# Pooled attention and a maxout network: when the third and fourth batches' queries are turned by DMA, and when the fourth k is folded

## The chip, the cores and the metric

The kernel runs on one core of one Trainium2 chip. The metric is the device time of one execution in microseconds, as a median of several runs. The profile is of one execution; its span is a little shorter than the device time.

A core has TensorE (PE, matrix products, with PEld for its weight loads), VectorE (DVE), ScalarE (ACT), GpSimd (POOL) and SyncE (SP). Each takes its instructions in the order of the program and waits for semaphores of others. DMA transfers are issued here by GpSimd (all loads but the first k), by SP (stores, and transposes during a DMA) and in one place by ScalarE.

## The reference

There are 8 batches of 8 heads, 576 positions and 64 dimensions. Keys and values are averaged over groups of 8 positions, so each head has 72 keys. Attention with these is followed by a network whose hidden layer is the largest of three products.

```python
k_p = k.reshape(B, H, Sp, pool, D).mean(axis=3)      # Sp = 72, pool = 8
v_p = v.reshape(B, H, Sp, pool, D).mean(axis=3)
scores = scale * np.matmul(q, k_p.transpose(0, 1, 3, 2))
attn = softmax(scores)                               # written out in the reference
attn_out = np.matmul(attn, v_p)

x = attn_out.transpose(0, 2, 1, 3).reshape(B * S, H * D)      # 4608 x 512
h = np.maximum(np.maximum(x @ w1, x @ w2), x @ w3)            # 4608 x 768
return h @ w_out                                              # 4608 x 512
```

## The kernel before

The network works on blocks of 512 rows (`block(n, ...)`, n from 0), while the attention of a later batch is woven in between its products. A block is a row of slots: each slot is one product of the network, and a plan says which attention steps follow it. In the steps, b is the batch (0 is the first): `q0` to `q3` turn a quarter or so of the queries on TensorE, `T` turns all of a batch's queries in one DMA transpose, `k` turns the folded keys, `s0` to `s7` are the scores of a head, `v` the products with the values, `x` turns their result.

```python
def load_q(b):
    qbs[b] = ld.tile([128, 4, NG, D], BF16, name="qb", tag="qb")     # two buffers
    src = ...
    n = 2 if b == 0 else 4
    for i in range(0, 4, n):
        nc.gpsimd.dma_start(out=qbs[b][:, i:i + n], in_=src[:, i:i + n])

def fold(e, t, out, dtype=F32):          # sums of 8, in three steps
    ...
    e.tensor_tensor(out=f, in0=t[:, :, 0:4, :], in1=t[:, :, 4:8, :], op=ALU.add)
    e.tensor_tensor(out=f[:, :, 0:2, :], in0=f[:, :, 0:2, :], in1=f[:, :, 2:4, :], op=ALU.add)
    e.tensor_tensor(out=out, in0=f[:, :, 0, :], in1=f[:, :, 1, :], op=ALU.add)

def turn_q(b, n0, n1, evac, tag):
    ...
    for n in range(n0, n1):
        nc.tensor.transpose(pqt[:, n - n0, :], qf[:, 128 * n:128 * n + 128], ident)   # line 182
    evac(out=qTs[b][:, n0:n1, :], in_=pqt)                                            # line 184

def turn_k(b):
    pkt = keys(b, ...)                   # three transposes, line 189
    for par, evac in enumerate((nc.vector.tensor_copy, nc.scalar.copy)):
        for odd in range(2):
            (evac if b > 2 else nc.vector.tensor_copy)(      # line 198; up to b = 2 all four on VectorE
                out=kz_all[b % 2][par][64 * par:64 * par + 64, :, 0:Sp]...[:, :, :, :, odd],
                in_=pkt[64 * odd:64 * odd + 64]...)

def score(b, h, out, tp, i0, i1):
    f = NG * (h // 2) + tp
    n = f // 2
    nc.tensor.matmul(out, kz_all[b % 2][f % 2][:, h, :],                              # line 207
                     qTs[b][:, n + i0:n + i1, 64 * (h % 2):64 * (h % 2) + 64], ...)

def scores(b, h):                        # two products, of kz of even and of odd parity
    psc = psum([128, 1024], F32, name="psc", tag="att", bufs=2)
    score(b, h, psc[:, 192:512], 0, 0, 5)
    score(b, h, psc[:, 512:768], 1, 0, 4)
    exp(ets[b][:, h, :], psc[0:Sp, 192:768])

# in do(b, steps):
    elif name[0] == "T":
        qTs[b] = sb2.tile([128, 2 * NG, 128], BF16, name="qT", tag="qT")
        nc.sync.dma_start_transpose(                                                  # line 289
            out=qTs[b], in_=qbs[b].rearrange("p hp t d -> p (hp t d)"))

def hidden_part(n, jc, c0, c1, hT):
    for wi in range(1, 3):
        pw = psum([128, c1 - c0], F32, name=f"pw{wi}", tag="pw", bufs=3)
        for kc in range(KCH):
            mm = nc.tensor.matmul(pw, w_sb[wi][...], xT[:, kc, col], ...)             # line 346
        if wi == 1:
            nc.scalar.activation(out=t, in_=pw, func=FT.Relu)
        else:
            nc.vector.tensor_tensor(out=hT[:, jc, c0:c1], in0=t, in1=pw, op=ALU.max)  # line 354
        yield                            # end of a slot
```

In block 1 the slots 0 to 11 are products of 256 columns, 12 to 17 of 512; then come eight slots of the output (lines 391 and 395). The even ones of the hidden slots are emptied by ScalarE, the odd ones by VectorE.

Of the kernel before, what the change touches and what calls it, by code (L numbers as in the profile page):

```python
# [14 lines left out]
def kernel(  # L15
# [11 lines left out]
    nc = tc.nc  # L27
# [37 lines left out]
    kts, vts, qbs, kps, qTs, ets = {}, {}, {}, {}, {}, {}  # L65

    def after(loads, first):
        for x in loads:
            tc.add_manual_dep(x.ins, first.ins.name, mybir.DependencyInfo(
                mybir.DependencyClass.Sync, mybir.DependencyReason.DATA),  # L70
                reason="weights first")
# [10 lines left out]
    def load_v(b, eng, dtype=F16, cuts=(0, H)):  # L82
        if b == 0:
            vts[0] = ld.tile([96, 4096], dtype, name="vt0", tag="vt")[:, 0:3072].rearrange(
                "p (h i d) -> p h i d", h=H, i=6)
            src = v[0].rearrange("h (p i) d -> p h i d", i=6)
            return [eng.dma_start(out=vts[0][:, h:g], in_=src[:, h:g])
                    for h, g in zip(cuts, cuts[1:])][-1]
        vts[b] = ld.tile([Sp, H, POOL, D], dtype, name="vt", tag="vt")
        src = v[b].rearrange("h (sp j) d -> sp h j d", j=POOL)  # L90
        return [eng.dma_start(out=vts[b][:, h:g], in_=src[:, h:g])
                for h, g in zip(cuts, cuts[1:])][-1]

    def load_q(b):
        qbs[b] = ld.tile([128, 4, NG, D], BF16, name="qb", tag="qb")
        src = q[b].rearrange("h s d -> (h s d)").rearrange(
            "(hp p t d) -> p hp t d", hp=4, p=128, t=NG)
        n = 2 if b == 0 else 4
        for i in range(0, 4, n):
            nc.gpsimd.dma_start(out=qbs[b][:, i:i + n], in_=src[:, i:i + n])  # L100

    w_sb = [const.tile([128, KCH, DFF], F16, name=f"mw{wi}", tag=f"mw{wi}")
            for wi in range(3)]
# [19 lines left out]
    for sign in (1, -1):  # L123
        nc.gpsimd.affine_select(
            out=pick, in_=pick, compare_op=ALU.is_ge, fill=0.0, base=7 * (sign < 0),
            pattern=[[sign, 6], [-8 * sign, 128]], channel_multiplier=6 * sign)
    for i in range(3):
        load_w(slice(256 * i, 256 * i + 256))
    nc.gpsimd.dma_start(
        out=wo_sb, in_=moe_w_out.rearrange("(jc p) c -> p jc c", p=128))  # L130
# [16 lines left out]
    def fold(e, t, out, dtype=F32):  # L147
        part, n = t.shape[:2]
        f = const.tile([part, n, 4, D], dtype, name="half" if dtype == F32 else "halfh",
                       tag="half" if dtype == F32 else "k16")  # L150
        e.tensor_tensor(out=f, in0=t[:, :, 0:4, :], in1=t[:, :, 4:8, :], op=ALU.add)  # L151
        e.tensor_tensor(out=f[:, :, 0:2, :], in0=f[:, :, 0:2, :], in1=f[:, :, 2:4, :],  # L152
                        op=ALU.add)
        e.tensor_tensor(out=out, in0=f[:, :, 0, :], in1=f[:, :, 1, :], op=ALU.add)

    def new_kp(b):
        kps[b] = sb2.tile([96, 6, D], BF16, name="kp", tag="kp")

    def fold_k(b, e, i0=0, i1=6):
        if b not in kps:  # L160
            new_kp(b)
        fold(e, kts[b][:, i0:i1], kps[b][:, i0:i1], F16 if e is nc.vector else F32)

    def fold_v(b):
        fold(nc.gpsimd, vts[b], vp_all[:, b, :, 0:D])
# [9 lines left out]
    def turn_q(b, n0, n1, evac, tag):  # L175
        if b not in qTs:
            qTs[b] = sb2.tile([128, 2 * NG, 128], BF16, name="qT", tag="qT")
        pqt = psum([128, n1 - n0, 128], BF16, name="pqt", tag=tag[0],
                       bufs=tag[1])
        qf = qbs[b].rearrange("p hp t d -> p (hp t d)")  # L180
        for n in range(n0, n1):
            nc.tensor.transpose(pqt[:, n - n0, :], qf[:, 128 * n:128 * n + 128],  # L182
                                ident)
        evac(out=qTs[b][:, n0:n1, :], in_=pqt)  # L184
# [9 lines left out]
    def turn_k(b):  # L194
        pkt = keys(b, ATT if len(pools) < 3 else SC)
        for par, evac in enumerate((nc.vector.tensor_copy, nc.scalar.copy)):
            for odd in range(2):
                (evac if b > 2 else nc.vector.tensor_copy)(  # L198
                    out=kz_all[b % 2][par][64 * par:64 * par + 64, :, 0:Sp].rearrange(
                         "p h (r i t) -> p h r i t", i=3, t=2)[:, :, :, :, odd],  # L200
                     in_=pkt[64 * odd:64 * odd + 64].rearrange("p i (h r) -> p h r i", r=12))
# [12 lines left out]
    def new_et(b):  # L214
        ets[b] = sb2.tile([Sp, H, S], F16, name="et", tag="et")
# [57 lines left out]
    PW = ("pw", 3)  # L273

    QS = ((0, 5), (5, 10), (10, 14), (14, 18))
    xns, mms = {}, []

    def do(b, steps):

        for name in steps.split():
            i = int(name[1:] or 0)
            if name[0] in "qQ":
                turn_q(b, *QS[i], nc.vector.tensor_copy if name[0] == "Q"
                       else nc.scalar.copy, TR)
            elif name[0] == "T":
                qTs[b] = sb2.tile([128, 2 * NG, 128], BF16, name="qT", tag="qT")
                nc.sync.dma_start_transpose(
                    out=qTs[b], in_=qbs[b].rearrange("p hp t d -> p (hp t d)"))  # L290
            elif name[0] == "k":
                turn_k(b)
            elif name[0] == "K":
                fold_k(b, nc.vector)
            elif name[0] == "s":
                if i == 0:
                    new_et(b)
                (scores if len(pools) < 3 else scores_flat)(b, i)
            elif name[0] == "d":
                sub_w(i)  # L300
            elif name[0] == "z":
                for par in range(2):
                    nc.vector.memset(kz_all[1][par], 0.0)
            elif name[0] == "w":
                turn_w(i, nc.scalar.copy if i % 2 else nc.vector.tensor_copy)
            elif name[0] == "v":
                xns[b, i] = values(b, CHUNKS[i][0])
            else:
                turn_x(b, *CHUNKS[i], xns[b, i], TR if b == 1 else ATT,
                       nc.vector.tensor_copy if name[0] == "X" else nc.scalar.copy)  # L310
# [4 lines left out]
    def sub_w(i, j0=0, j1=2, wi=(1, 2)):  # L315

        part = slice(256 * i + 128 * j0, 256 * i + 128 * j1)
        for t in [w_sb[w] for w in wi]:
            nc.vector.tensor_tensor(out=t[:, :, part], in0=t[:, :, part],  # L319
                                    in1=w_sb[0][:, :, part], op=ALU.subtract)  # L320
# [177 lines left out]
    def block(n, plan, parts, folds=()):  # L498

        for slot, _ in enumerate(part for stage in parts for part in stage(n)):  # L500
            if slot == 0 and n > 0:
                pool_work(n, mms[-1])
            for b, steps in plan.get(slot, ()):
                if b < B:
                    do(b, steps)
            if folds and slot in FOLDS:
                next(folds.pop(0))
# [3 lines left out]
              17: [(1, "K")], 24: [(1, "q0 k")], 25: [(1, "q1")],  # L511
              26: [(1, "s0 q2")], 27: [(1, "s1 s2")], 28: [(1, "s3 Q3")],
              29: [(1, "s4 s5")], 30: [(1, "s6 s7")], 31: [(1, "v0")],
              32: [(1, "v1 x0")], 33: [(1, "X1 v2 v3")]}, (hidden, project))
    load_k(3, nc.gpsimd)
    load_v(3, nc.gpsimd)
    load_q(3)
    fold_k(2, nc.gpsimd)
    fold_v(2)


    def plan1():
        return {1: [(1, "x2")], 2: [(1, "v4")], 3: [(1, "x3")],
                5: [(1, "x4")],
                6: [(2, "k")], 7: [(2, "q0")], 9: [(2, "q1")], 11: [(2, "q2 s0")],
                12: [(2, "s1 q3")], 13: [(2, "s2")], 14: [(2, "s3")], 15: [(2, "s4"), (3, "T")],
                16: [(2, "s5")], 18: [(2, "s7")],
                19: [(2, "v0")],
                20: [(2, "v1 x0")], 21: [(2, "v2 x1")], 22: [(2, "v3 x2")],
                23: [(2, "v4 x3")], 24: [(2, "x4"), (4, "T")], 17: [(2, "s6")]}  # L530
# [6 lines left out]
        got[14 if n == 2 else 13].append((b + 2, "T"))  # L537
        return got

    FOLDS_OF = {1: "k3 v3", 2: "k4 v4 k5", 3: "v5 k6 v6", 4: "k7 v7"}  # L540

    def pool_work(n, mm):

        if n + 3 < B:
            if n == 1:
                load_q(4)
            after([load_k(n + 3, nc.gpsimd)], mm)
            load_v(n + 3, nc.gpsimd)
            if n > 1:
                load_q(n + 3)  # L550
        for name in FOLDS_OF.get(n, "").split():
            if name[0] == "k":
                fold_k(int(name[1]), nc.gpsimd)
            else:
                fold_v(int(name[1]))
# [231 lines left out]

    folds = [f for wi in range(1, 3) for f in [fold_w(wi)] * 4]
    block(1, plan1(), (hidden, project))
    for n in range(2, 5):  # L790
        block(n, with_keys(n) if n == 5 - 1 else plan(n),
              (hidden, project))
# [50 lines left out]
```

The softmax here doesn't subtract the row's maximum and nothing guards it: scores larger than these inputs give would overflow.

## Time and profile before

| | before |
|---|---|
| device time, median of 3 | 230.81 us (230.67 to 230.87) |
| span of the profile | 229.0 us |
| TensorE busy | 219.8 us, 96% |
| VectorE busy | 130.5 us, 57% |
| ScalarE busy | 122.6 us, 54% |
| GpSimd busy | 140.0 us, 61% |
| moved by DMA | 33.52 MB |

The page gives for each engine its busy time and its share of the span. A second part follows the chain of work that ended last from the last instruction back to the first; the share of an engine in it tells more than its busy time. The timeline prints, in order of time, the start and the length of merged instructions, the engine, the line of the kernel, what is written and what is read, and in brackets how long the engine stood idle before and what ended that. A name such as `DMA_TRANSPOSE` on SPq is the time of issue on the queue; the time to landing is given apart.

### The profile page before, as it was taken

What the parts mean: (1) busy time and instruction counts of PE and PEld (TensorE: products, weight loads), DVE (VectorE), ACT (ScalarE), POOL (GpSimd) and SP (SyncE); (2) the same over time, 40 slices, a digit from 0 to 9 for tenths busy, and PEclk for the clock granted to TensorE, in tenths of its full rate; (3) what the DMA queues carried; (4) which work ended last, traced back from release to release, by engine and by line L of the source; (5) the groups of instructions that cost most, each with busy time, mean ns of one, the idle gap of its engine ahead of it and who ended that gap; (6) DMA issues with size and microseconds to landing.
All of it is one profiled execution on the core that took longest, in us unless ns stands there. A gap on an engine that the chain in (4) does not pass through costs nothing.

```text
span 229.0 us, 4411 instructions
## 1 busy us (share of the span) xinstructions
PE 219.8 (96%) x1686; PEld 134.9 (59%) x1687; DVE 130.5 (57%) x246; ACT 122.6 (54%) x221; POOL 140.0 (61%) x115
## 2 busy tenths in 40 slices
PE   7888999999999999999999999999999999999992
PEld 2477645568655545544554455455677667786682
DVE  3668876048426423632363236368578887897830
ACT  2277425756864586238623852683776435465330
POOL 7975201999959999999999759900343443920020
PEclk9999999999999999999999999999999999999999
DMA  6999999999569999986998799941421534301326
GB/s 172 208 197 197 211 202 208 194 177 225 106 110 216 221 161 212 159 194 119 223 153 199 127 218 189 190 110 24 92 53 40 121 71 87 84 11 46 76 68 183
DMA packets 47157, 33.52 MB, mean 146 GB/s; under 512 B 27104, under 2 KB 41888, under 8 KB 47136
## 3 DMA queue, kind: packets, MB, share of 16 engines
q0 software_dynamic: 16944, 16.98, 46.0%
q1 hardware_dynamic: 30032, 16.13, 32.2%
q8 instruction: 13, 0.21, 0.4%
q10 hardware_dynamic: 160, 0.13, 0.2%
q14 instruction: 8, 0.07, 0.1%
HBM read 34.60 MB, written 9.44 MB: 192 GB/s over the span
## 4 chain that ended last, share of the span: by engine, by line
PE 88%; DVE 6%; ACT 3%; issue 2%; DVEq 0%; ACTq 0%
PE pw L346 23%; PE po L395 18%; PE po L391 11%; PE pA L733 7%; PE psc L207 6%; PE pav L255 4%; PE pC L733 3%; PE wm L413 3%; PE pm L333 2%; PE oA L670 2%; PE pB L733 2%; DVE kz L198 2%; PE pqt L182 2%; DVE xn L263 2%; ACT kz L198 2%
## 5 line engine op out<-in xcount | busy, mean ns | idle before, releaser
L346 PE MATMUL pw<-xT,mw 128*128 128x512 f16 (+1 forms) x336 | 73.1, 349 | 0.4 <-ACT xT L249 0.2
L395 PE MATMUL po<-mwo,hT 128*128 128x512 f16 (+1 forms) x198 | 46.8, 373 | 0.0
L354 DVE TENSOR_TENSOR hT<-t,pw 128x512 f16<-128x512 f16 (+1 forms) x42 | 25.5, 610 | 36.7 <-ACT et L212 22.3
L346 PEld LDWEIGHTS <-mw 128*128 128x128 f16 x336 | 31.6, 98 | 21.5 <-DVE mw L319 0.6
L400 ACT COPY osb<-po 128x512 f32<-128x512 f32 (+1 forms) x32 | 18.5, 579 | 41.2 <-PE po L395 41.1
L212 ACT ACTIVATE et<-psc 72x576 f16<-72x576 f32 (+2 forms) x54 | 35.2, 660 | 7.1 <-PE psc L207 6.9
L151 POOL TENSOR_TENSOR half<-vt 72x2048 f32<-72x2048 f16 x7 | 28.4, 4060 | 14.1 <-DMA vt<-in_v_dram 13.7
L391 PE MATMUL po<-wm,xT 128*128 128x512 f16 (+1 forms) x132 | 33.0, 372 | 0.3 <-ACT osb L400 0.3
L352 ACT ACTIVATE t<-pw 128x512 f16<-128x512 f32 (+1 forms) x42 | 22.5, 537 | 13.4 <-PE pw L346 11.6
L263 DVE TENSOR_TENSOR xn<-pav,rcp 128x512 f16<-128x512 f32 x40 | 27.7, 691 | 1.6 <-DVE rcp L261 0.2
L395 PEld LDWEIGHTS <-hT 128*128 128x128 f16 x198 | 18.5, 98 | 16.3
L152 POOL TENSOR_TENSOR half<-half 72x1024 f32<-72x1024 f32 (+1 forms) x13 | 27.3, 2097 | 1.0
L207 PE MATMUL psc<-qT,kz 128*128 128x320 bf16 (+2 forms) x120 | 22.9, 278 | 1.8 <-DVE qT L184 0.9
L207 PEld LDWEIGHTS <-kz 128*128 128x128 bf16 x143 | 13.1, 98 | 14.7 <-ACT kz L198 2.0
L151 POOL TENSOR_TENSOR half<-ktFalse 96x1536 f32<-96x1536 f16 x6 | 18.6, 3099 | 4.3 <-DMA ktFalse<-in_k_dram 4.1
L255 PEld LDWEIGHTS <-et 72*128 72x128 f16 x320 | 15.4, 98 | 7.6 <-issue 0.3
L739 ACT CAST pad<-pA 128x512 f16<-128x512 f32 x27 | 15.3, 587 | 8.4 <-PE pA L733 6.0
L261 DVE RECIPROCAL rcp<-pav 128x8 f32<-128x8 f32 x40 | 8.2, 206 | 18.1 <-PE pav L255 17.9
L391 PEld LDWEIGHTS <-xT 128*128 128x128 f16 x132 | 12.1, 98 | 9.4 <-issue 0.4
L255 PE MATMUL pav<-vp,et 72*128 72x65 f16 x320 | 17.0, 194 | 0.1
L714 DVE SCALAR_TENSOR_TENSOR hT<-pad 128x512 f16<-128x512 f16 x18 | 14.4, 810 | 1.8 <-ACT pad L743 1.4
L733 PEld LDWEIGHTS <-sw 128*128 128x128 f16 x144 | 13.7, 98 | 2.7
(106 smaller groups left out, 279.2 us busy)
## 6 DMA issues: line engine op xcount, KB each, us to landing
out_dram<-osb SPq DMA_DIRECT2D x62, 128.0 KB, 3.2
ktFalse<-in_k_dram POOLq DMA_DIRECT2D x7, 576.0 KB, 6.6
qb<-in_q_dram POOLq DMA_DIRECT2D x7, 576.0 KB, 13.2
vt<-in_v_dram POOLq DMA_DIRECT2D x7, 576.0 KB, 10.9
mw<-in_moe_w_dram POOLq DMA_DIRECT2D x9, 256.0 KB, 9.2
ktTrue<-in_k_dram SPq DMA_DIRECT2D x3, 384.0 KB, 5.0
mwo<-in_moe_w_out_dram POOLq DMA_DIRECT2D x1, 768.0 KB, 13.2
qb<-in_q_dram POOLq DMA_DIRECT2D x2, 288.0 KB, 7.8
```

What stands on the lines that cost most here:

```text
L151: e.tensor_tensor(out=f, in0=t[:, :, 0:4, :], in1=t[:, :, 4:8, :], op=ALU.add)
L152: e.tensor_tensor(out=f[:, :, 0:2, :], in0=f[:, :, 0:2, :], in1=f[:, :, 2:4, :], op=ALU.add)
L207: nc.tensor.matmul(out, kz_all[b % 2][f % 2][:, h, :], qTs[b][:, n + i0:n + i1, 64 * (h % 2):64 * (h % 2) + 64], start=True, stop=True)
L212: nc.scalar.activation(out=out, in_=in_, func=FT.Exp, scale=1.0 / 64.0)
L255: nc.tensor.matmul(pav[:, h // 4, 65 * (h % 4):65 * (h % 4) + 65], ets[b][:, h, c0:c0 + 128], vp_all[:, b, h, :], start=True, stop=True)
L263: nc.vector.tensor_tensor(out=xn, in0=pv[:, :, :, 0:D], in1=rcp.to_broadcast([128, 2, 4, D]), op=ALU.mult)
L346: mm = nc.tensor.matmul(pw, w_sb[wi][:, kc, bass.ts(jc, 128)], xT[:, kc, col], start=(kc == 0), stop=(kc == KCH - 1))
L352: nc.scalar.activation(out=t, in_=pw, func=FT.Relu)
L354: nc.vector.tensor_tensor(out=hT[:, jc, c0:c1], in0=t, in1=pw, op=ALU.max)
L391: nc.tensor.matmul(po, xT[:, kc, bass.ts(m, 128)], wm_sb[:, kc, c], start=(kc == 0), stop=False)
L395: nc.tensor.matmul(po, hT[:, jc, bass.ts(mm, 128)], wo_sb[:, jc, c], start=False, stop=(jc == JCH - 1))
L733: mm = nc.tensor.matmul(p[:, w], a[:, kc, bass.ts(g, 128)], b[:, kc, :], start=(i in FIRST and w + kc == 0), stop=(w + kc == 2), skip_grou ...
```

## The change

The queries of the third batch (b = 2), which TensorE turned in four groups in block 1, are turned by one DMA transpose, issued by SP in block 0. The loads of the fourth batch are put behind it: the query load waits until that transpose has landed, and the k and v loads follow on the same queue. The fold of the third k comes ahead of these loads. The DMA transpose of the fourth batch (b = 3) waits until the v load has landed, and the query load of the fifth waits for that transpose. So both transposes run at times when no load is under way. To make room for these waits, GpSimd's work of block 1 is written down at slot 16 rather than at slot 0, and the fold of the fourth k is taken out of it and put ahead of the loads of the fifth batch. The key turn of the third batch moves from slot 6 to slot 7.

```diff
--- before.py
+++ after.py
@@ -96,8 +96,8 @@
         src = q[b].rearrange("h s d -> (h s d)").rearrange(
             "(hp p t d) -> p hp t d", hp=4, p=128, t=NG)
         n = 2 if b == 0 else 4
-        for i in range(0, 4, n):
-            nc.gpsimd.dma_start(out=qbs[b][:, i:i + n], in_=src[:, i:i + n])
+        return [nc.gpsimd.dma_start(out=qbs[b][:, i:i + n], in_=src[:, i:i + n])
+                for i in range(0, 4, n)][-1]
 
     w_sb = [const.tile([128, KCH, DFF], F16, name=f"mw{wi}", tag=f"mw{wi}")
             for wi in range(3)]
@@ -273,7 +273,7 @@
     PW = ("pw", 3)
 
     QS = ((0, 5), (5, 10), (10, 14), (14, 18))
-    xns, mms = {}, []
+    xns, mms, turned = {}, [], {}
 
     def do(b, steps):
 
@@ -286,8 +286,10 @@
                        else nc.scalar.copy, TR)
             elif name[0] == "T":
                 qTs[b] = sb2.tile([128, 2 * NG, 128], BF16, name="qT", tag="qT")
-                nc.sync.dma_start_transpose(
+                turned[b] = nc.sync.dma_start_transpose(
                     out=qTs[b], in_=qbs[b].rearrange("p hp t d -> p (hp t d)"))
+                if b == 3:
+                    after([turned[b]], last_v)
             elif name[0] == "k":
                 turn_k(b)
             elif name[0] == "K":
@@ -498,7 +500,7 @@
     def block(n, plan, parts, folds=()):
 
         for slot, _ in enumerate(part for stage in parts for part in stage(n)):
-            if slot == 0 and n > 0:
+            if slot == (16 if n == 1 else 0) and n > 0:
                 pool_work(n, mms[-1])
             for b, steps in plan.get(slot, ()):
                 if b < B:
@@ -511,19 +513,20 @@
               17: [(1, "K")], 24: [(1, "q0 k")], 25: [(1, "q1")],
               26: [(1, "s0 q2")], 27: [(1, "s1 s2")], 28: [(1, "s3 Q3")],
               29: [(1, "s4 s5")], 30: [(1, "s6 s7")], 31: [(1, "v0")],
-              32: [(1, "v1 x0")], 33: [(1, "X1 v2 v3")]}, (hidden, project))
+              32: [(2, "T"), (1, "v1 x0")], 33: [(1, "X1 v2 v3")]}, (hidden, project))
+    fold_k(2, nc.gpsimd)
+    after([load_q(3)], turned[2])
     load_k(3, nc.gpsimd)
-    load_v(3, nc.gpsimd)
-    load_q(3)
-    fold_k(2, nc.gpsimd)
+    last_v = load_v(3, nc.gpsimd)
     fold_v(2)
+    fold_k(3, nc.gpsimd)
 
 
     def plan1():
         return {1: [(1, "x2")], 2: [(1, "v4")], 3: [(1, "x3")],
                 5: [(1, "x4")],
-                6: [(2, "k")], 7: [(2, "q0")], 9: [(2, "q1")], 11: [(2, "q2 s0")],
-                12: [(2, "s1 q3")], 13: [(2, "s2")], 14: [(2, "s3")], 15: [(2, "s4"), (3, "T")],
+                7: [(2, "k")], 11: [(2, "s0")],
+                12: [(2, "s1")], 13: [(2, "s2")], 14: [(2, "s3")], 15: [(2, "s4"), (3, "T")],
                 16: [(2, "s5")], 18: [(2, "s7")],
                 19: [(2, "v0")],
                 20: [(2, "v1 x0")], 21: [(2, "v2 x1")], 22: [(2, "v3 x2")],
@@ -537,13 +540,13 @@
         got[14 if n == 2 else 13].append((b + 2, "T"))
         return got
 
-    FOLDS_OF = {1: "k3 v3", 2: "k4 v4 k5", 3: "v5 k6 v6", 4: "k7 v7"}
+    FOLDS_OF = {1: "v3", 2: "k4 v4 k5", 3: "v5 k6 v6", 4: "k7 v7"}
 
     def pool_work(n, mm):
 
         if n + 3 < B:
             if n == 1:
-                load_q(4)
+                after([load_q(4)], turned[3])
             after([load_k(n + 3, nc.gpsimd)], mm)
             load_v(n + 3, nc.gpsimd)
             if n > 1:
```

## The prediction

> **What bounds the kernel now.** I read the chain that ended last first, then the same chain cut to the stretch that the diff edits, then the timelines of VectorE, GpSimd and the SP queue over that stretch.
>
> ```profile
> PE 88%; DVE 6%; ACT 3%; issue 2%; DVEq 0%; ACTq 0%
> ```
>
> The chain is TensorE for 88% of the span. The table of stretches says the same for the second block alone (51.4 to 77.5 us): TensorE is busy 25.97 of 26.10 us. So in this block a TensorE instruction taken away is worth its time, unless a wait lay behind it. The chain, start and length in us, from the third batch's keys to its second score:
>
> ```profile
> 55.59 0.13 PE pkt L189 x3
> 55.72 0.44 PE pw L346 x4
> 56.16 0.28 PE pqt L182 x5
> 56.44 0.87 PE pw L346 x8
> 57.31 0.36 PE pqt L182 x5
> 57.68 0.09 issue
> 57.76 0.43 DVE hT L354
> 58.20 0.04 issue
> 58.24 0.60 PE pw L346 x4
> 58.84 0.22 PE pqt L182 x4
> 59.06 0.25 PE psc L207 x2
> 59.31 0.86 PE pw L346 x4
> 60.17 0.24 PE psc L207 x2
> 60.41 0.22 PE pqt L182 x4
> ```
>
> The four pqt pieces are the 18 transposes to be removed. Between 57.68 and 58.24 the chain leaves TensorE: a hidden product waits until VectorE has emptied a PSUM tile. Why VectorE was late is in its timeline:
>
> ```profile
> 55.76 1.97 DVE L198 COPY kz<-pkt 64x288 bf16<-64x288 bf16 x4 [0.30 <-PE pkt L189]
> 57.76 0.75 DVE L354 TENSOR_TENSOR hT<-t,pw 128x256 f16<-128x256 f16 x2
> ```
>
> Four key copies hold VectorE for 1.97 us, and two maxima queue behind them. The weight-load row shows the real idle time of TensorE there as 0.31 us. This point decides how much of the saving is kept. Last, the queues:
>
> ```profile
> 47.09 0.55 POOL L79 DMA_DIRECT2D ktFalse<-in_k_dram  x1
> 49.26 3.12 POOL L151 TENSOR_TENSOR half<-ktFalse 96x1536 f32<-96x1536 f16 x1
> 65.96 0.77 POOL L100 DMA_DIRECT2D qb<-in_q_dram  x1 [2.71 <-DMA qT<-qb]
> ```
>
> ```profile
> 61.45 1.99 SPq L289 DMA_TRANSPOSE qT<-qb  x1
> 76.56 5.31 SPq L289 DMA_TRANSPOSE qT<-qb  x1
> ```
>
> The DMA transpose at 61.45 starts when the loads have landed and needs 1.99 us of issue and 4.0 us to landing (the tile view's minimum is 3.9). The one at 76.56 runs beside loads: 5.31 us of issue, 7.4 us to landing. GpSimd waited 2.71 us for the first of them. None of these is on the chain.
>
> [...] Thus a load that waits for a transpose holds all of GpSimd behind it; the 2.71 us above is such a case.
>
> **The change part by part.**
>
> *Removed from TensorE: 18 transposes.* By the chain's pieces 0.28 + 0.28 + 0.22 + 0.22 = 1.00 us (the second piece reads 0.36, of which I take 0.28, as the first, which has the same five; the rest is already the stall). Their busy time by line is 1.66 us, but those spans overlap in the pipeline, so I use the chain. Their weight loads run beside matmuls. On ScalarE four copies go, 2.55 us; ScalarE has idle time throughout this block, so that is worth nothing by itself.
>
> *Moved: the third batch's key turn, from slot 6 to slot 7, and the gap after it shortened.* The instruction order of the changed kernel shows one VectorE maximum now ahead of the four key copies, and the order on TensorE becomes: hidden product 7, keys, products 8 to 11, then score 0, whose two weight loads wait for VectorE. I lay it out from the end of product 6 (55.59), with durations of the trace:
> - Product 7 to 56.03, keys to 56.16, products 8 to 11 (4 x 0.435) to 57.90. Product 10 needs the maximum of product 7, done by about 56.7: no wait there any more.
> - VectorE: maximum 7 from 56.29, the copies from about 56.65, each 0.495. The first two (even parity) end at 57.64, the last (odd) at 58.62.
> - Score 0's first half needs the even copies: 57.90 to 58.04. Its second half needs the odd ones: it waits from 58.04 to 58.62, some 0.6 us. With 0.05 for the semaphore and the 0.28 that such a restart took at 80.80 ("PE psc", behind the same kind of copy), product 12 starts at 58.95.
> - Before, product 12 started at 59.31, and one more transpose group of 0.22 followed after score 1. Thus the gain is 59.31 - 58.95 + 0.22 = 0.58 us.
>
> In words: the transposes filled part of the time in which TensorE must wait for the key copies anyway. Of 1.00 us, about 0.6 us of new wait less the 0.3 us of old wait, and the restart, takes away 0.4.
>
> *Added: one DMA transpose, of the third batch.* In SP order it stands after the stores of the third output tile of the first block; those are issued from 48.37, for 1.18 us. So it is issued near 49.55. The fourth batch's three loads, issued at 47.09 to 48.48 before, now wait for it, so it runs against two stores and perhaps the last of an earlier load (third batch's values, issued 24.82 and landed after the largest time in the tile view, 24.1, at 48.9). I take 4.0 us: landed at 53.6. Score 0 would use it at 57.90, a margin of 4.3 us. Even the loaded 7.4 us would be in time (57.0).
>
> *Moved on GpSimd.* The third k fold goes ahead of the loads: from 47.09, three operations with gaps, 6.0 us as before (49.26 to 55.34), to 53.1. Then it waits for the transpose: landing 53.6 plus the 0.5 us seen at 65.96, so about 54.1. Three issues of 0.77, 0.54 and 0.85 bring 56.3; the v fold lasts 7.8 us, to 64.1. Its reader, the first value product, stood at 68.42 and would come at 67.8: margin 3.7 us. The fourth k fold follows, to 70.1.
>
> *The fourth batch's transpose now waits for its v load.* Three loads need 12.4 to 14.5 us (the group at 65.96 to 67.25 landed 5.7, 8.1 and 14.5 us after issue), so v lands at 67 to 70 and the transpose at 71 to 74. Its reader, the first score in the third block, stood at 80.80: margin 6 us or more. The output stores of the second block queue behind it from 69.2, by up to 3 us, with five output tiles to spare.
>
> *The fifth batch's loads* come at 71.5 to 74.5 instead of 65.96. The v fold of the fourth batch then ends at 81.5 to 84.5 (82.1 before), 7 us or more ahead of its use near 91. The fifth batch's query transpose starts later than 76.56 and still beside loads, to land by about 88; it is used near 103. After that GpSimd is where it was.
>
> Sum: -0.58 us on TensorE, everything else beside it. 230.81 - 0.6 = 230.2 us. Behind the second block TensorE is on the chain nearly without a break, and queue work follows TensorE, so I expect the gain to reach the end.
>
> **Rivals.**
> - *The full saving.* If the key copies don't hold score 0 for 0.6 us (a different order, or copies done earlier), TensorE keeps 1.00 us, and with the old 0.3 us stall gone too 1.3 us: 229.5 to 229.8. For it: the maximum of product 7 is no longer behind the copies. Against it: 1.97 us of copies behind a product that ends 1.9 us ahead of score 0.
> - *The wait for the DMA takes its place.* If the transpose is issued later than 49.55, or lands 8 us after issue, score 0 waits, GpSimd's loads slip too, and the v fold at 64.1 eats its 3.7 us. A landing at 60 would cost 2 us and make 232. Against it: 4.0 us was measured for one alone.
> - *The fourth batch's chain is too tight.* Transpose behind v, loads behind the transpose, folds behind loads: were each 3 us late, the first score of block three would still be fed. I see at most 0.5 us there: about 230.7.
> - *Nothing stays*, since the moved key turn costs all of it: 230.8. My layout would have to be wrong by 0.6 us in VectorE's copies.
>
> **Range and chances.** My working gives 230.2. The full saving sets the low end, 229.6; the high end, 230.8, is the case in which the new wait swallows it all. The runs before lie within 0.2 us, which adds little. Two per cent is 4.6 us, more than all the TensorE time that is removed; a slowing so large needs a transpose that lands over 8 us late. So: faster by over 2% 0.01, within 2% 0.98, slower 0.01.
>
> **What would show it.** In the changed profile: 36 transposes of line 182 instead of 54; in the chain, a stretch at score 0 of the third batch that leaves TensorE for the VectorE copies of line 198, about 0.6 us; the new DMA transpose issued near 49.6 and landed in about 4 us; GpSimd's loads from about 54; no wait of a score for a DMA transpose, none of a value product for GpSimd. The prediction is wrong if TensorE waits for a query transpose, or if the chain passes through GpSimd, or if the key copies don't show and the whole 1.0 us is kept.

## The result and the profile after

| kernel | median us | lowest and highest |
|---|---|---|
| before | 230.92 | 230.67 to 231.05 |
| changed | 249.88 | 248.32 to 255.58 |

The ratio is 1.080, with an interval of 1.077 to 1.083: slower by 19 us, where 0.6 us less was predicted. Ratios and intervals in this document leave out executions over 1.5% above the fastest one of the same kernel (here 252.60 and 255.58 us); the medians leave out none. Executions of the changed kernel spread from 243.2 to 255.6 us, of which more below. The profile read here is of an execution of 243.23 us (span 241.5, before 229.0), which lost less than the median; of one of 255.58 us single numbers are given.

The chain that ended last, by engine:

```profile
PE 78%; DMA 8%; DVE 5%; ACT 2%; issue 2%; POOL 1%; SPq 1%; DVEq 0%; POOLq 0%; ACTq 0%
```

DMA, absent from this line before, now holds 8% of the span. The same chain shows where (start, length, what):

```profile
4.68 8.76 DMA vt<-in_v_dram
...
97.48 1.71 SPq L239
...
99.28 11.51 DMA xT<-xn
110.79 0.09 issue
110.88 1.86 PE pw L348 x4
```

The first of the two is the load of the first batch's values, at the start of the program. It has little to do with the loss: the copy behind the first value products starts at 14.33, before at 14.15. The second is the loss. TensorE has no work from 99.96 to 110.88: the network's fourth block cannot start, because its input xT, the turned attention result, is still on its way. The three transposes issued ahead of it took 15.2, 15.7 and 11.5 us from issue to landing; the same three took 4.5, 3.0 and 2.4 us before. The list of waits puts 10.9 us on this one wait, and in the execution of 255.58 us 22.9 us. The restart is slow too: four products in 1.86 us, where four took 0.86.

As a ledger, from the same instructions in both traces: the key turn of the fourth batch comes 0.56 us earlier than before (77.82 against 78.38); the first product after the wait 10.4 us later (110.88 against 100.51), and the product behind the next first score 12.2 us later (116.15 against 103.91). The spans differ by 12.5. So nearly all of the loss is this wait and the slow restart behind it; the second block did bring a gain.

What delays xT begins with the fifth batch's query transpose. The SP queue, each line with its start and time of issue:

```profile
49.85 2.34 SPq L289 DMA_TRANSPOSE qT<-qb  x1
...
68.08 1.82 SPq L289 DMA_TRANSPOSE qT<-qb  x1
...
79.01 8.72 SPq L289 DMA_TRANSPOSE qT<-qb  x1
...
94.69 8.89 SPq L239 DMA_TRANSPOSE xT<-xn  x2
```

The first two are the transposes that the change is about, and they are as quick as planned. The third is one that the change does not mention: 76.56 and 5.31 us of issue before. Then it stood behind stores until 76.45, with its queries landed since 71.7 (65.96 + 5.7). Now SP waits for these queries (75 to 85 us; us in total, times, longest):

```profile
SPq L289 <- DMA qb<-in_q_dram: 3.0, 1, 3.0
```

From 82 to 84 us the queues look as follows. The queue lines give the packets that started, MB and the share of the 16 engines' time; the others are the issues in this time, with KB and us from issue to landing. q0 carries the loads of GpSimd, the fifth batch's values among them (issued at 73.82, landed at 89.2); q1 carries the transposes and stores of SP.

```profile
q0 software_dynamic: 259, 0.26, 80.2%
q1 hardware_dynamic: 158, 0.04, 40.5%
...
ktFalse<-in_k_dram POOLq DMA_DIRECT2D x1, 576.0 KB, 18.3
vt<-in_v_dram POOLq DMA_DIRECT2D x1, 576.0 KB, 23.3
qb<-in_q_dram POOLq DMA_DIRECT2D x1, 576.0 KB, 26.3
qT<-qb SPq DMA_TRANSPOSE x1, 23.6
```

The kernel before, at the end of the same transpose (81.5 to 83.5 us):

```profile
q1 hardware_dynamic: 1825, 0.46, 103.7%
q0 software_dynamic: 14, 0.09, 65.1%
...
ktFalse<-in_k_dram POOLq DMA_DIRECT2D x1, 576.0 KB, 6.4
...
qT<-qb SPq DMA_TRANSPOSE x1, 7.4
```

Read the packets, not the shares. A query transpose writes 128 x 2304 x 2 bytes, 0.59 MB; in the kernel before, the one at 61.45, which runs alone, shows 2336 packets with 0.59 MB, so about 250 bytes each (2304 of 256 bytes would be 0.59 MB). Of the one at 76.56, 1825 packets, four fifths, went in 1.65 us (33 of the 40 slices of that window) beside 14 load packets, some 1,100 per us. In the changed kernel the values' load is still running, and the transpose goes at 79 packets per us. From 88 to 90 us it is much worse:

```profile
q1 hardware_dynamic: 67, 0.02, 110.6%
q0 software_dynamic: 4, 0.02, 5.9%
```

71 packets in two microseconds, while 16 engines count as occupied. I call this the jam: a transpose packet takes 0.5 us (110.6% of 16 x 2 us by 67), where it took 0.02 before (103.7% by 1825), and nearly no bytes go. It begins about 87 us, when the first packets of 2 KB and more appear (none of 480 from 84 to 86 us, 2 of 614 from 86 to 88); by their size they are probably those of the sixth batch's key load, issued at 82.48. The three loads issued from 82 us, the stores at 87.82 and the three xT transposes take some 9 to 14 us longer to land than before. TensorE's wait ends when these loads are through: the last of the three xT transposes lands at 110.8, 0.6 us after the sixth batch's queries (83.88 + 26.3 = 110.2). In the four other traces with a wait of TensorE for xT at this place it lands 0.5 to 0.9 us after them too.

### The profile page after: what moved, and what is told of

It is laid out like the page before. It is cut to its first block, busy times and chain, and to the rows that moved or that the text cites. A ratio compares the mean times of both kernels' runs of the same rounds, so it can differ in the third digit from the quotient of the medians.

```text
span 253.9 us, 4375 instructions
## 1 busy us (share of the span) xinstructions
PE 220.7 (87%) x1668; PEld 134.4 (53%) x1669; DVE 130.4 (51%) x246; ACT 120.6 (48%) x217; POOL 140.1 (55%) x115
## 4 chain that ended last, share of the span: by engine, by line
PE 76%; DMA 7%; DVE 6%; SPq 6%; ACT 2%; issue 1%; DVEq 0%; ACTq 0%
PE pw L348 23%; PE po L397 15%; PE po L393 10%; PE pA L736 6%; PE psc L207 5%; DMA xT<-xn 5%; SPq L239 4%; PE pav L255 4%; PE pC L736 3%; DMA ktTrue<-in_k_dram 2%; PE pm L335 2%; PE oA L673 2%; DVE xn L263 2%; PE pB L736 2%; DVE kz L198 1%
## 5 line engine op out<-in xcount | busy, mean ns | idle before, releaser
L348 PE MATMUL pw<-xT,mw 128*128 128x512 f16 (+1 forms) x336 | 75.2, 357 | 23.2 <-DMA xT<-xn 22.9
L348 PEld LDWEIGHTS <-mw 128*128 128x128 f16 x336 | 32.2, 99 | 45.7 <-DMA xT<-xn 23.3
L356 DVE TENSOR_TENSOR hT<-t,pw 128x512 f16<-128x512 f16 (+1 forms) x42 | 25.5, 610 | 37.8 <-ACT et L212 22.9
L151 POOL TENSOR_TENSOR half<-vt 72x2048 f32<-72x2048 f16 x7 | 28.4, 4061 | 13.8 <-DMA vt<-in_v_dram 13.6
L263 DVE TENSOR_TENSOR xn<-pav,rcp 128x512 f16<-128x512 f32 x40 | 27.7, 691 | 1.6 <-DVE rcp L261 0.2
L198 DVE COPY kz<-pkt 64x288 bf16<-64x288 bf16 x18 | 8.6, 480 | 34.8 <-PE pkt L189 34.6
L207 PEld LDWEIGHTS <-kz 128*128 128x128 bf16 x143 | 13.3, 98 | 15.2 <-ACT kz L198 1.3
## 6 DMA issues: line engine op xcount, KB each, us to landing
qb<-in_q_dram POOLq DMA_DIRECT2D x7, 576.0 KB, 15.2
```

The lines of the kernel that those rows point to most:

```text
L207: nc.tensor.matmul(out, kz_all[b % 2][f % 2][:, h, :], qTs[b][:, n + i0:n + i1, 64 * (h % 2):64 * (h % 2) + 64], start=True, stop=True)
L263: nc.vector.tensor_tensor(out=xn, in0=pv[:, :, :, 0:D], in1=rcp.to_broadcast([128, 2, 4, D]), op=ALU.mult)
L348: mm = nc.tensor.matmul(pw, w_sb[wi][:, kc, bass.ts(jc, 128)], xT[:, kc, col], start=(kc == 0), stop=(kc == KCH - 1))
```

## The experiments

The theories, in words; each expectation says what its own give. First: **mixing**, the fifth batch's query transpose (T4 from here on) in flight together with loads makes both slow. Second: **the new transposes**, the third or fourth batch's, cost the time directly. Third: **long rows**, the k load, with its large contiguous rows in SBUF, blocks the queues by itself. The sixth batch's loads are called k5, v5, q5.

### T4 taken out

```diff
+ if b == 4: nc.vector.tensor_copy(out=qTs[b], in_=qTs[3]); continue    # step "T"
```

The fifth batch's queries are not turned; VectorE copies the fourth's.

> The changed kernel, but the fifth batch's queries are not turned by a DMA: a VectorE copy of the fourth batch's turned queries takes their place (this leaves out the turning of the fifth batch's queries, and its scores are of other queries). All loads stay where they are. Theory A (the fifth batch's transpose, running beside the k, v and q loads of the sixth, is what jams the DMA engines): no wait of TensorE for xT near 100 us; 229.5 to 231.5 us. Theory B (the loads are late by 6 us, so they collide with the five xT transposes near 92 us whatever the query transpose does): xT transposes still slow, 238 to 250 us.

231.11 us (230.48 to 232.27) against 230.80; ratio 1.0012, interval 1.0001 to 1.0023. The three xT transposes are back to 3.6, 3.8 and 3.0 us. So the whole loss hangs on T4; the two transposes that the change times anew are still there, and cost nothing that shows without it. The saving does not show, and the copy itself is in the way: 3.84 us on VectorE at 75.03, behind which the key copies of the fourth batch come late (TensorE waits 0.23 and 0.74 us).

### The sixth batch's loads wait for T4

```diff
- after([load_k(n + 3, nc.gpsimd)], mm)
+ x = load_k(n + 3, nc.gpsimd); after([x], mm)
+ if n == 2: after([x], turned[4])
```

> The changed kernel, but the sixth batch's k load (and so its v and q loads behind it) waits until the fifth batch's query transpose has landed. That transpose then runs beside the fifth v load alone. Theory A1 (three loads or any load beside a transpose for long jams): the transpose lands near 87, the loads then run from 87 to 101 beside the xT transposes from 92, which jam again: 235 to 250 us. Theory A2 (only loads that were issued while a query transpose was in flight jam it): no jam, 230 to 232 us.

238.59 us (238.23 and 238.94), ratio 1.032, interval 1.027 to 1.037. From 82 to 84 us only the fifth batch's values are loaded beside T4:

```profile
q0 software_dynamic: 237, 0.24, 71.7%
q1 hardware_dynamic: 222, 0.06, 40.4%
...
qT<-qb SPq DMA_TRANSPOSE x1, 10.7
```

That is about one transpose packet for one load packet. From 84 to 86 us:

```profile
q0 software_dynamic: 208, 0.21, 66.1%
q1 hardware_dynamic: 323, 0.08, 54.0%
```

In both stretches together 445 load packets and 545 transpose packets start, and the share moves between them (in the changed kernel 259 to 158, then 205 to 275). A load packet has 1.0 KB here and a transpose packet 0.26 KB, so the transpose gets a fifth to a little over a quarter of the bytes: 111 to 162 packets per us, a tenth to a seventh of the 1,100 it had alone. All 2304 beside a load would take 2304 / 162 to 2304 / 111, 14 to 21 us (an estimate from these rates). No jam follows, but the loads that were held back until 89.63 now run beside the xT transposes, which need 10 to 11 us, and TensorE waits 6.4 us. Holding loads back moves the meeting to the next transpose.

### Shorter rows for k, and the values ahead of k in the kernel before

```diff
 # in the changed kernel, tile of a k load: 4 elements of padding after each 1 KB row
- ld.tile([96, 6, POOL, D], ...)
+ ld.tile([96, 6, POOL * D + 4], ...)[:, :, 0:POOL * D].rearrange("p i (j d) -> p i j d", j=POOL)
 # in the kernel before, fifth batch
- after([load_k(4)], mm); load_v(4)
+ after([load_v(4)], mm); load_k(4)
```

> The changed kernel, but the k buffers have a gap of 4 elements after every 512, so that a k load goes in rows of 512 elements as the v load does, and not in rows of 3072. Same bytes. Theory C (the jam is due to the long rows of the k load, packets of some 6 KB, beside packets of 256 B of the transpose): the query transpose of the fifth batch slows down as it does beside the v load (about 140 packets in a us) and lands near 93 to 96; no collapse to 30 to 90 packets in a us; 230 to 236 us. Theory A (any loads in number): as the changed kernel, 247 to 252 us.

> The kernel before, with one exchange: the fifth batch's v load is issued ahead of its k load, so that the query transpose issued near 76.5 meets the tail of a k load instead of the tail of a v load. Theory C (long rows of k jam a transpose): the transpose, 7.4 us to landing before, takes 15 us or more, and the time rises by 5 us or more. Theory A (what counts is how many loads are in flight for how long): 7 to 9 us to landing, 230.5 to 231.5 us.

With the split rows: 243.36 us (241.49 and 245.24), between the two ranges expected. T4 still needs 19.0 us and k5 17.6, TensorE waits 9.0 us for xT. From 88 to 90 us there are now 305 transpose and 19 load packets in place of 67 and 4, so the jam is less deep, but it is there. Long rows are not needed for the loss, and that theory falls; with them the jam was deeper. With k's load put last in the kernel before: 230.86 us (230.24 to 231.12), ratio 0.9988, T4 6.9 us. This run says less than it was meant to, for T4 hardly met the long rows. From 76 to 79 us, and from 80 to 83 us:

```profile
q0 software_dynamic: 64, 0.37, 64.3%
q1 hardware_dynamic: 241, 0.23, 43.2%
...
q1 hardware_dynamic: 2253, 0.65, 112.0%
q0 software_dynamic: 1, 0.00, 0.0%
```

When nearly all of T4's packets went, k's were over. What long rows alone do to a transpose is not shown.

### In the kernel before, T4 issued when the values have landed

```diff
+ if b == 4: after([x], v4_load)       # x is the DMA transpose of step "T"
```

> The kernel before, with nothing of the change; only the fifth batch's query transpose waits until the fifth v load has landed (near 82 us), so that it meets the three loads of the sixth batch, issued from 82. Theory A (this meeting makes the loss): the query transpose needs 15 us or more to landing instead of 7.4, the xT transposes behind it are late, 238 to 252 us. Rival (the loss needs the added transpose or the moved GpSimd work): 230.5 to 231.5 us.

Ten executions gave 230.66, 230.72, 230.79 and 230.83, and 237.31, 237.63, 237.82, 238.25, 239.09 and 239.71 us; before on the same chip 230.70. By the four alone the ratio is 0.9999, with an interval of 0.998 to 1.002: the same. The trace is of 230.66: T4 issued at 81.31, 4.75 us later than before, landed 9.3 us after issue, k5 8.5. So T4 and all three loads (issued from 81.86 to 83.25) were in flight together there, and nothing was lost: the meeting alone does not make the jam each time. The other six lose 7 to 9 us, while none of 17 executions of the kernel before on that chip took over 231.76. That fits a meeting that jams only sometimes, but it is not shown, as there is no trace of one of the six.

### The new transpose alone, and the new order without it

```diff
 # on the kernel before: third batch by DMA, loads where they were
+ 32: [(2, "T"), ...            - q0 to q3 of batch 2; k to slot 7
 # on the changed kernel: third batch turned on TensorE again
- 32: [(2, "T"), ...            + q0 to q3 of batch 2; k at slot 6
- after([load_q(3)], turned[2]) + load_q(3)
```

> One part of the change alone on the kernel before: the third batch's queries turned by DMA, and its key turn at slot 7; loads and folds as before, so the transpose (near 49.6) runs beside the fourth batch's loads. Theory A (a transposed packet goes for each load packet while both run): some 15 to 25 us to landing, near 65 to 70, and TensorE waits at the third batch's first score from 58: 237 to 243 us. Rival (a single query transpose beside loads costs 7.4 us as seen before): landing at 57, 230.0 to 230.5 us.

> The changed kernel with its new order of loads and folds and its waits, but the third batch's queries turned by TensorE as before, so that no DMA transpose is added and the fourth batch's loads start when GpSimd comes to them, near 53. Theory A1 (what counts is that loads start 6 us late, behind the k fold; the added transpose costs only 1 us more): the fifth batch's transpose meets the sixth batch's loads all the same, 238 to 252 us. Theory A2 (the added transpose itself takes the DMA time that is then missing): 230.5 to 232 us.

The transpose alone: 237.27 us (236.82 and 237.73), ratio 1.028, interval 1.024 to 1.032. It is issued at 50.02, behind loads issued from 46.84 to 48.23, lands after 13.8 us, and the third batch's first score waits (the last figures are the idle time of TensorE and what ended it):

```profile
63.82 0.64 PE L207 MATMUL psc<-qT,kz 128*128 128x320 bf16 x2 [5.88 <-DMA qT<-qb]
```

So the waits that the change puts around its loads are needed. The order without the transpose: 243.81 us (242.88 and 244.74), ratio 1.054, interval 1.048 to 1.060. GpSimd's timeline, then SP's:

```profile
52.96 0.79 POOL L99 DMA_DIRECT2D qb<-in_q_dram  x1
```

```profile
76.64 11.95 SPq L289 DMA_TRANSPOSE qT<-qb  x1
```

The k fold put first makes the fourth batch's loads 5.9 us later (47.09 before), the fifth batch's follow at 70.72 (65.96 before), and T4 falls among them: 11.95 us of issue, 23.5 to landing; k5, v5 and q5 need 19.6, 24.7 and 27.7 us, and TensorE waits 10.1 us for xT. The full jam, without the added transpose. The theory of the new transposes falls; it is the new order of loads and folds.

### The changed kernel again

> The changed kernel once more, for its profile: 248 to 252 us, with the fifth batch's query transpose some 25 us or more in flight, from 78.

243.23 and 253.44 us, one below the expected range and one above it, on a chip where before took 230.70; T4 took 23.6 us in the first, which is the execution shown above.

### The later query transposes put where no load runs

```diff
 # first version, on the changed kernel
- got[...].append((b + 2, "T"))            + got[...].append((b + 1, "T"))    # and (4, "T") out of block 1
 n == 1:      q4 (after turned[3]), k4 (after mm), v4, k5
 n in (3, 4): v of n + 2 (after the block's last xT transpose), q of n + 2, k of n + 3
 n == 5:      q7, v7
 # folds v6 and v7 follow their loads; (7, "T") comes in the last block
 # second version: v of n + 2 after mm in place of the xT transpose; q7 after mm
 # third version
 n == 2:      v5
 n in (3, 4): k of n + 3 (after mm), q of n + 2, v of n + 3
 n == 5:      q7
```

> The changed kernel with its loads laid out anew so that no load runs beside a query transpose from the fifth batch on, nor beside the xT transposes except at an edge: the fifth batch's query transpose moves to slot 14 of the third block, the next three to the block after, the sixth k goes with the fifth batch's loads, and the later loads wait until the xT transposes of the batch before have landed. Theory A (the loss is nothing but transposes beside loads): no wait of TensorE for xT, the 0.6 to 0.8 us saved in the second block reach the end: 230.0 to 230.3 us. Rival (the new order of loads, or GpSimd's later folds, costs as much): 231 us or more, with a wait for the last k or v fold near 158 us.

> The new lay-out of loads once more, but the later loads start at the first product of their block, as in the kernel before, and no longer wait for the last xT transposes of the batch before. In the run with that wait the first jam, near 78 to 122 us, was gone, and a new one stood at 143, where the seventh batch's query transpose met loads that started at 129. Theory A: loads start near 123 and are through by 138, the transpose issued near 140 takes about 4 us, and the time is 230.0 to 230.6 us. Rival (loads beside the xT transposes of the batch before jam them too): 234 us or more.

> The last lay-out had no jam, but its eighth v fold on GpSimd, at 161 to 169, stood beside VectorE's subtractions of line 606, which took 3.7 and 2.5 us there and 0.9 after the fold had ended; 3.0 us of it was a wait of TensorE. Here the v loads are brought forward by one place (the sixth v behind the fourth v fold, the eighth with the seventh batch's), so that all folds end near 147. Theory A: nothing of the jam, nothing of this wait, and the saving of the second block is kept: 229.7 to 230.4 us. Rival (four loads at a time run beside the xT transposes and jam): 232 us or more.

First version: 240.41 us (238.86 to 241.46), ratio 1.043, interval 1.040 to 1.046. T4, now at 98.43 without loads, has 2.05 us of issue; but the seventh batch's transpose, at 143.04, meets loads issued from 129.1 and lands after 6.6 us, and TensorE waits 1.4, 1.5 and 0.6 us for transposes, 3.5 of the 8.1 us by which the span is longer than before. The rest was not followed, and the time is far from the 230.0 to 230.3 us expected. Second: 236.81 us (235.99 to 237.63), ratio 1.024, interval 1.021 to 1.028. No transpose jams any more; two scores wait 0.6 and 0.7 us for queries. The largest loss left is another thing, a wait of 3.0 us for VectorE's subtractions (VectorE, then GpSimd):

```profile
161.72 3.73 DVE L606 TENSOR_TENSOR pad<-xT 128x512 f16<-128x512 f16 x1 [0.77 <-DMA xT<-xn]
...
169.27 0.88 DVE L606 TENSOR_TENSOR pad<-xT,pad 128x512 f16<-128x512 f16 x1
```

```profile
161.12 4.05 POOL L151 TENSOR_TENSOR half<-vt 72x2048 f32<-72x2048 f16 x1 [10.30 <-DMA vt<-in_v_dram]
```

The eighth v fold has slid into the last block's work, and a VectorE subtraction beside it takes 3.73 us, against 0.88 after it. Third version, with v earlier: 230.42 us (230.12 to 231.99), ratio 0.9994, interval 0.9974 to 1.0013. T4 has 2.09 us of issue at 98.59 and 4.0 to landing; no jam. The same subtraction, with GpSimd idle:

```profile
160.46 0.41 DVE L607 TENSOR_TENSOR pad<-xT 128x512 f16<-128x512 f16 x1
```

The loss is gone; a gain over the kernel before is not shown. Transposes and loads were both moved here, so the run does not say which of the moves was needed.

### The third version without the third batch's DMA transpose

The edit is that of the order without it, above, on the third version.

> The same lay-out, but the third batch's queries turned by TensorE as before. Theory A (the added DMA transpose gives the saving, the lay-out only lets it through): 0.6 to 0.9 us above the run with it, 230.5 to 231.0 us. Rival (the lay-out itself brings the gain): as fast as the run with it.

231.21 us (230.66 to 231.43), ratio 1.0014, interval 1.0007 to 1.002. By the medians the DMA transpose brings 231.21 - 230.42 = 0.8 us in this layout, and by the spans 229.5 - 228.7 = 0.8 us. Five of the fourteen times of the third version lie above 231.1, so the size is less certain than the two figures look. The layout itself costs about 0.3 us (the ratio 1.0014); where, was not followed.

## Why the prediction was wrong

Right, by the steps of the text:

- *The third batch's DMA transpose*: issued 49.85 (predicted 49.55), landed after 4.2 us (4.0). GpSimd's loads at 54.65 (54.1); end of the v fold 64.7 (64.1), of the fourth k fold 70.9 (70.1).
- *The key copies.* The chain of the changed kernel at the third batch's first score:

```profile
57.68 0.46 DVE kz L198
...
58.16 0.49 DVE kz L198
58.65 0.05 issue
58.70 0.28 PE psc L207
58.98 0.86 PE pw L348 x4
```

  It leaves TensorE for the copies where the layout put it, and product 12 starts at 58.98 (58.95). That the two agree so well is luck. This execution was 0.20 us behind the kernel before when the block's work began to differ (the same product at 55.19 and 54.99) and 0.56 us ahead at the fourth batch's keys, so the block gained 0.76 us, where 0.58 was predicted; in the execution of 255.58 us it gained 0.75. The copies began earlier than laid out: at 56.67, less those 0.20, where the layout had 56.65.
- *The fourth batch's transpose* at 68.08, landed after 3.9 us, and the fifth batch's loads from 72.49: inside the ranges given.

```profile
54.65 0.79 POOL L99 DMA_DIRECT2D qb<-in_q_dram  x1 [1.50 <-PE pxt L245]
...
72.49 0.79 POOL L99 DMA_DIRECT2D qb<-in_q_dram  x1 [1.56 <-DMA qT<-qb]
```

  The bracket of the first line names a transpose on TensorE that ended about then; the DMA transpose for which the load waits landed at 54.1.

Wrong were two sentences in "The fifth batch's loads": that T4 "starts later than 76.56 and still beside loads, to land by about 88", and "After that GpSimd is where it was". It landed at 102.6, and in the execution of 255.58 us, where it needed 35.7 us, at 114. Three errors lie in it.

- *What 7.4 us meant.* I took it as the cost of a transpose beside loads. But four fifths of that transpose, 1825 packets, went in 1.65 us with the loads at 14 packets. That 7.4 us is the time beside loads was my estimate, and is not shown. Beside one load for all of its length T4 would need 14 to 21 us by the estimate above.
- *The transfers slid by different amounts.* The loads went from 65.96 to 72.49, 6.5 us; T4, which had 4.9 us of slack between the landing of its queries and its issue, only from 76.56 to 79.01. The values' load had ended at 81.8 before (67.25 + 14.5), 5.2 us after T4's issue. By my own range for q4, 71.5 to 74.5, it would end at 87 to 90; it ended at 89.2, 10.2 us after T4's issue. The numbers for that were in the text, and I did not lay this transfer out as I had laid out VectorE.
- *The sixth batch's loads did not slide at all.* The issue of the fifth batch's values and of the sixth batch's keys, before and then changed:

```profile
67.25 0.85 POOL L91 DMA_DIRECT2D vt<-in_v_dram  x1
82.05 0.55 POOL L79 DMA_DIRECT2D ktFalse<-in_k_dram  x1
...
73.82 0.86 POOL L91 DMA_DIRECT2D vt<-in_v_dram  x1
82.48 0.55 POOL L79 DMA_DIRECT2D ktFalse<-in_k_dram  x1
```

  Before, the fourth batch's k fold and v fold lay between the two, 14.8 us, about as long as the v load takes to land (14.5). The change puts the k fold ahead of the fifth batch's loads, which leaves the v fold and 8.7 us. So "After that GpSimd is where it was" is right for the time and misses what it means: the next loads now come 6.7 us before the v load has landed. No run moves this fold alone, so how much of the loss it carries beside the later start is not shown.

From this follows the failed sum, "everything else beside it". The page of the kernel before has a row of DMA share by slice:

```profile
DMA  6999999999569999986998799941421534301326
```

With 9 in most slices up to 150 us there is nearly always a transfer in flight, which was a reason to lay them all out. It does not say that the queues are full: the jam has 110.6% with 67 packets and 0.02 MB, and the third version above moves these loads and loses nothing. None of the rivals had a transfer that the diff leaves alone become the bound; the rival "the fourth batch's chain is too tight" followed that chain to the score, and not to T4.

What is shown, and what is not: that T4 must be there (taken out, the loss is gone), that the new order of loads and folds brings the full loss without the added transpose, and that moving the query transposes away from loads, with a new order of loads, removes it. That a later T4 alone brings a loss is suggested by six of ten executions and not shown. About one transpose packet for one load packet (222 to 237) goes with a T4 of 10.7 us. The jam, 67 packets in 2 us, is not explained by it. In the traces of 243.23 and 255.58 us k5's loads were issued while T4 was in flight; from 88.0 to 88.5 us of the second, 1 load packet starts and 5.9% of the 16 engines' time goes to loads, 0.5 us, and 13 transpose packets have 97.1%, 0.6 us each. Why so few go is open, and so is why the same meeting passed without a jam in the 230.66 us above. Open too is what makes the jam deeper in one execution than in another, 243 to 256 us.

## What to carry to other kernels

Before moving a load or a DMA transpose, lay out the queue like an engine: which transfers are in flight together before and after, by packets per us, and what each waits for: its own data, the instructions ahead of it on its queue, or another engine. Work that is moved away from between two loads brings the loads together (here from 14.8 to 8.7 us). The duration of a transpose "beside loads" says nothing until the packets show how much of it ran beside them. Where several executions of one kernel spread while its neighbour's do not, look at which transfers meet in it.

## What was unexpected of the hardware

- A DMA transpose beside loads falls from about 1,100 to between 79 and 162 packets per us, and in the jam to about 33; the loads suffer too (k5 6.4 to 18.3 us).
- A VectorE subtraction that reads and writes SBUF alone took 3.73 us beside GpSimd's add (second version) and 0.41 with GpSimd idle (third version); the first ended at 165.45, just after the add at 165.17 (161.72 + 3.73 and 161.12 + 4.05). The bf16 copy without T4 took 3.84 us from 75.03; there the changed kernel has an add of 4.07 us on GpSimd, from 74.70. No run has the copy alone. A key copy, which reads PSUM, kept its time: 0.49 us beside an add of 4.06 (before, at 55.76) and 0.48 with GpSimd idle (second version, at 159.99). Why the subtraction is so long is not shown.
- After 10.9 us without work TensorE is slow for a while: four products in 1.86 us, eight in 2.92, then 0.86 for four again from 116.15. The granted clock is 0.80 as a mean from 96 to 110.88 us, 0.84 from there to 125 us and 1.00 after that; the kernel before has 1.00 from 96 us to the end. What lowers it is not shown. It cost some 1.9 us here: from the first product to the one behind the next first score it is 5.27 us (110.88 to 116.15), before 3.40 (100.51 to 103.91).
